# The first batch's mirror image added by the transfer that brings it, and transfers moved between engines, in a fused FFT and two-layer-pair kernel

## Chip, cores and metric

The kernel runs on one core of a Trainium2 chip. The metric is device microseconds of that core for one execution. Five engines take part: PE (TensorE, matrix products; PEld in the profile is its loading of weights), DVE (VectorE), ACT (ScalarE), POOL (GpSimd) and SP (SyncE, which only issues transfers here). Each engine works through its own list of instructions in order; a transfer (DMA) is issued by one engine's list and carried by 16 shared DMA engines. SP and ACT issue through one kind of queue, POOL through another.

## What is computed

The input x is 4 batches of 3008 rows by 256 columns, all float32. The parts of the reference that matter:

```
X = np.fft.fft(x, axis=1);  X = np.fft.fft(X, axis=2);  x = X.real      # (4, 3008, 256)
h = x @ w_in;   r = np.maximum(h, 0.0);  x = (r * r) @ w_out            # 256 -> 2048 -> 256
h = x @ w_in2;  x = (h * np.cos(h)) @ w_out2                            # 256 -> 2048 -> 256
```

The weights of both layer pairs arrive as float64 and are turned into pairs of float32r numbers (a high and a low part) on the chip. A product is then three matmuls: high by high, high by low, low by high.

## The kernel before

The transform along the rows uses its symmetries. For each batch and each of three row tiles t (128 partitions) two arrays of 128x1024 float32 (512 KB each) are loaded: one of row pairs a, and one of their mirror images b. `fold_steps` (line 230) then works in place on DVE: `mirrored` adds b to a (one 128x1024 instruction); two `eo` steps write sums and differences of even and odd parts (128x512 each); two `half` steps (128x512 each) write the next level; `hi` copies one half of the result into a float32r tile dh on ACT, `lo` writes the remainder dl on DVE; two `quarter` steps (128x256 each) and a second `hi` and `lo` do the other half. PE multiplies dh and dl by cosine and sine tables (`transform`, line 305; tables `tabs`, six tiles of 752 or 756 KB, loaded by POOL at line 206 with a conversion to float32r). A middle column of 128 rows goes the same way in small (`load_128`, `fold_128`, `job_128`). `finish` and `finish_first` turn the products into the rows z of the first layer's input (ACT, DVE, POOL) and store them to DRAM; the first two blocks of batch 0 stay on the chip as xh and xl.

The columns' transform is folded into the first layer's weights: `conv_w1` converts a chunk of w_in in eight steps (ACT and DVE), `dft_w1` multiplies it by the table cs on PE (line 416), `split_w1` splits the product into wah and wal.

Layer pair 1 runs in blocks of up to 512 pairs of tokens (12 blocks) by 16 slices of the hidden dimension: `l1_mm1` (line 527, six matmuls), `l1_add` (DVE: one multiply-add and two sums), `l1_act` (ACT: three passes), `l1_lo` (POOL, four instructions, line 557), `l1_mm2` (line 569, twelve matmuls, three steps later). Batches 1 to 3 are loaded, folded and transformed between those steps. The tables' tiles serve as landing place of the next batch's x in between, so the tables are loaded again for each batch (`reload_tab`, by POOL). Layer pair 2 works on 24 halves of blocks with eight steps each: `l2_mm1` (line 621), range reduction and cosine on ACT and DVE, `l2_lo` on POOL (line 660), `l2_mm2` (line 672); `l2_out` copies the sums out of PSUM, one half by ACT and one by DVE into one tile o, and stores both by SP.

The order of all this is written out by hand: every step is an entry `at(time, step, name)`; the dictionary `TIMES` (line 71) overrides the times of named entries, and the entries are issued in order of time. The time is only a sort key; what counts is the order that results on each engine. Before the first entry that runs on PE, for instance, SP issues the two halves of the first chunk of w_in, the middle column and the six arrays of batch 0 in one go, and POOL issues cs and all six tables. In the steady part POOL issues the loads of z (`load_z`), of the second layer's input (`load_o`), of the converted second weights (`load_w2`) and of the tables between its `l1_lo` and `l2_lo` instructions; SP issues everything else.

Of the kernel before, what the change touches and what calls it, by code (L numbers as in the profile page):

```python
# [10 lines left out]
F32 = mybir.dt.float32  # L11
# [5 lines left out]
AF = mybir.ActivationFunctionType  # L17
ALU = mybir.AluOpType
# [3 lines left out]
P = 128  # L22
# [8 lines left out]
NT = 3  # L31
# [5 lines left out]
BLK = 512  # L37
# [7 lines left out]
HALVES = [(2 * c + n * w, w) for c, w in BLOCKS for n in range(2)]  # L45
# [12 lines left out]
TW = (2 * J_A, EES + J_EE + 1)  # L58
# [15 lines left out]
class Order:  # L74
# [5 lines left out]
    def at(self, t, fn, name=None):  # L80
        self.ops.append((TIMES.get(name, t), len(self.ops), fn))

# [6 lines left out]
def f32(ap):  # L89
    return ap.bitcast(F32)  # L90
# [3 lines left out]
def kernel(ctx: ExitStack, tc: tile.TileContext, x, x128, cs, tab0, tab1, w_in1, w_out1, w_in2, w_out2, out):  # L94
    nc = tc.nc
# [10 lines left out]
    at = od.at  # L106
# [12 lines left out]
    def buf(tag, name, dt=F32, pool=work, bufs=1, shape=(P, 2, BLK)):  # L119
        return pool.tile(list(shape), dt, name=name, tag=tag, bufs=bufs)  # L120
# [35 lines left out]
    def from_f64(st, hi, lo, sh=None):  # L156
# [36 lines left out]
        def lower():  # L193
            r, unit = (w1.bitcast(F32), 2.0 ** -20) if middle is None else (middle, 2.0 ** -36)
            v.scalar_tensor_tensor(out=lo, in0=r, scalar=unit, in1=got["a"].bitcast(F32), op0=ALU.mult, op1=ALU.mult)

        return [size, guard, mask, merge, rest, power] + [join] * (middle is None) + [lower]


    raws, dat, jobs = {}, {}, {}  # L200
    tabs = [[buf(f"t{i}{t}", f"t{i}{t}", F32R, fft, 1, (P, 2, TW[i])) for t in range(NT)] for i in range(2)]
    cs_sb = []
    u128 = [buf(f"u128{p}", f"u128{p}", F32R, fft, 1, (P, 4, NT, B)) for p in "hl"]

    def load_tab(i, t):
        nc.gpsimd.dma_start(out=tabs[i][t], in_=(tab0, tab1)[i][t])

    def reload_tab(i, t):
        tabs[i][t] = buf(f"t{i}{t}", f"t{i}{t}", F32R, fft, 1, (P, 2, TW[i]))
        load_tab(i, t)  # L210

    def load_cs():
        cs_sb.extend(buf(f"cs{p}", f"cs{p}", F32R, fft, 1, (P, 2, D)) for p in "hl")
        for p, src in zip(cs_sb, cs):
            nc.gpsimd.dma_start(out=p, in_=src.rearrange("(k p) d -> p k d", p=P))

    def load_x(b, t, bufs):
        raws[b, t] = bufs
        for i, r in enumerate(bufs):
            nc.sync.dma_start(out=r, in_=x[b, t, i].rearrange("p a e d -> p (a e d)").rearrange("p (h n) -> p h n", h=2))  # L220

    def tt(out, in0, in1, op):
        nc.vector.tensor_tensor(out=out, in0=in0, in1=in1, op=op)  # L223

    PM = (ALU.add, ALU.subtract)
# [4 lines left out]
    def fold_steps(b, t):  # L230

        x = {}

        def views():
            ra, rb = raws.pop((b, t))
            x["a"], x["b"] = ra, rb
            x["eo"] = units(rb, "p (e a d) -> p e a d", e=2, a=4)

            x["f"] = units(ra, "p (i a b d) -> p i a b d", i=2, a=2, b=2)
            x["fv"] = units(ra, "p (a b d) -> p a b d", a=4, b=2)  # L240

            x["g"] = units(rb, "p (i a d) -> p i a d", i=4, a=2)

            x["src"] = (units(ra, "p (a n) -> p a n", a=4)[:, 1:3], units(rb, "p (a n) -> p a n", a=4)[:, 0:2])

        def mirrored():
            views()
            tt(x["a"], x["a"], x["b"], ALU.add)

        def eo(i):  # L250
            ab = units(x["a"], "p (a e d) -> p a e d", a=4, e=2)
            tt(x["eo"][:, i], ab[:, :, 0], ab[:, :, 1], PM[i])

        def half(i):
            tt(x["f"][:, i], x["eo"][:, :, 0::2], x["eo"][:, :, 1::2], PM[i])

        def quarter(i):
            tt(x["g"][:, i], x["fv"][:, 0:4:3, 0], x["fv"][:, 0:4:3, 1], PM[i])

        def hi(i):  # L260
            if i == 0:
                x["p"] = [buf(f"d{p}", f"d{p}", F32R, fft, NT, (P, 2, 2, 2 * P)) for p in "hl"]
                dat[b, t] = [p.rearrange("p a b (u d) -> p (a b u) d", d=P) for p in x["p"]]
            nc.scalar.activation(x["p"][0][:, i], x["src"][i], AF.Copy)  # L264

        def lo(i):
            tt(x["p"][1][:, i], x["src"][i], f32(x["p"][0])[:, i], ALU.subtract)

        return [mirrored] + [lambda i=i, fn=fn: fn(i) for fn, i in (
            (eo, 0), (eo, 1), (half, 0), (half, 1), (hi, 0), (lo, 0), (quarter, 0), (quarter, 1), (hi, 1), (lo, 1))]  # L270
# [11 lines left out]
    def load_128():  # L282
        raws["mid"] = scratch(2, NT, 4, B)
        nc.sync.dma_start(out=raws["mid"], in_=x128)
# [114 lines left out]
    def load_w1(c, bufs):  # L399
        for k, st in enumerate(bufs):  # L400
            nc.sync.dma_start(out=st.rearrange("p h n -> p (h n)").rearrange("p (n t) -> p n t", t=2),
                              in_=src_in(w_in1, k, c * FCH * P, FCH * P))
            wi[c, k] = st.rearrange("p h n -> p (h n)").rearrange("p (n t) -> p n t", t=2)
# [89 lines left out]
    def load_w2(name, c):  # L493
        parts = w_chunk("a" if name == "in" else "b")
        for p, src in zip(parts, w2_dram[name, c]):
            nc.gpsimd.dma_start(out=p, in_=src)
        (wi2 if name == "in" else wo2).append(parts)
# [16 lines left out]
    def load_z(k, i):  # L514
        c, w = BLOCKS[k]
        if i == 0:
            load_zb(k, x_buf())
        nc.gpsimd.dma_start(out=xt[1, k][i][:, :, :w], in_=z_dram[i][:, :, c:c + w].rearrange("i p w -> p i w"))
# [86 lines left out]
    def load_o(k):  # L605
        c, w = HALVES[k]
        parts = x_buf()
        for p, o in zip(parts, o_dram):
            nc.gpsimd.dma_start(out=p[:, :, :w], in_=o[:, :, c:c + w].rearrange("m p w -> p m w"))
        xt[2, k] = parts  # L610
# [64 lines left out]
    def l2_out(k):  # L675
        c, w = HALVES[k]
        o = buf("AB"[k % 2] + "0", "o")
        a = accs.pop((2, k))
        nc.scalar.activation(o[:, 0, :w], a[:, 0, :w], AF.Copy)
        nc.vector.tensor_copy(o[:, 1, :w], a[:, 1, :w])  # L680
        for m in range(2):
            nc.sync.dma_start(out=out[m][:, c:c + w], in_=o[:, m, :w])
# [42 lines left out]
    def fold(times, b, t):  # L725
        got = []

        def step(j):
            if j == 0:
                got.extend(fold_steps(b, t))  # L730
            got[j]()

        for j, when in enumerate(times):
            at(when, lambda j=j: step(j), ("fold", b, t, j))
# [15 lines left out]
    for t in range(NT):  # L750
        fold([-80 + t + 0.05 * j for j in range(7)] + [0.02 + 0.1 * t + 0.01 * j for j in range(4)], 0, t)
        for i, job in enumerate(JOBS[::2]):
            at(-79.5 + t + 0.01 * i, lambda t=t, i=i, job=job: start_first(job, ps_a, f"acc{i}", (t,)), ("T", 0, i, t))
        at(-79.45 + t, lambda t=t: job_128(0, (t,)), ("job_128", 0, t))
        at(-78.7 + 0.01 * t, lambda t=t: load_tab(1, t), ("tab", 1, t))
# [17 lines left out]
    t = 0.4  # L773
# [3 lines left out]
    for key in KEYS:  # L777
        span = 1.5
        if isinstance(key, tuple):
            c, k = key  # L780
            convert(t, span, key, lambda c=c, k=k: conv_w1(c, k))
            if k:
                end = t + span
                at(end, lambda c=c: dft_w1(c), ("dft", c))
                at(end + 0.1, lambda c=c: split_w1(c), ("split", c))
                at(end + 0.8, lambda c=c: load_wc(c), ("load_wc", c))
                if c < NCH - 1:
                    at(end + 0.01, lambda c=c: load_w1(c + 1, pair("B", I32)), ("load_w1", c + 1))
        else:
            convert(t, span, key, lambda f=key: conv_wo1(f))  # L790
            if key < NF - 4:
                at(t + span, lambda f=key + 4: load_wo1(f, buf(f"A{f // 2 % 2}", "wo", I32)), ("load_wo1", key + 4))
        t += span


    for b, (load, start, gap, t1, gap1) in {1: ((14, 21, 21.6), 26, 4, 38.4, 1.5), 2: ((53, 53.5, 54), 54, 4.6, 68, 2), 3: ((76, 76.5, 77), 78, 4.6, 92, 2)}.items():
        for t in range(NT):
            at(load[t], lambda b=b, t=t: load_x(b, t, staged(t)), ("load_x", b, t))
            fold([start + gap * t + gap / 11 * j for j in range(11)], b, t)
        for i in range(2):  # L800
            for t in range(NT):

                at(start + gap * ((i * NT + t) // 2 + 1) + 0.1, lambda i=i, t=t: reload_tab(i, t), ("tab", b, i, t))
        for i, job in enumerate(JOBS):
            def begin(b=b, job=job):
                jobs[b, job] = ps_h.tile([P, 2, BLK], F32, name="h")
                transform(job, jobs[b, job], lhs_of(b), P)

            at(t1 + gap1 * i + 0.2, begin, ("T", b, *job))
            finish(t1 + gap1 * i + 0.9, b, job, lambda b=b, job=job: jobs[b, job], lambda: pair("B", F32R), 0.3)  # L810
# [175 lines left out]
```

## Time and profile before

| | us |
|---|---|
| median of three runs | 1945.47 |
| lowest and highest run | 1945.16, 1946.25 |
| the profiled execution's own time | 1946.22 |
| its span, first to last instruction | 1944.4 |
| PE busy in the span | 1893.9 |
| DVE, ACT, POOL busy | 1361.7, 1482.8, 1139.8 |

The span is 1.8 us shorter than the time of the same execution; the rest lies around it. A busy time is the sum of an engine's instructions. The granted clock of a stretch is the share of full speed at which the throttle let TensorE run: 1.00 is 2.4 GHz, 0.50 is 1.2 GHz. Its mean over the span is 0.993.

### The profile page before, as it was taken

To read this page: it belongs to the slowest core of one execution; us is meant where nothing else is said; L and a number is where in the kernel's file an instruction comes from. 1 tells how busy PE (TensorE), PEld (TensorE's weight loads), DVE (VectorE), ACT (ScalarE), POOL (GpSimd) and SP (SyncE) were. 2 spreads that over 40 slices of the span, in tenths; PEclk is the share of its full clock that TensorE was granted. 3 is DMA by queue.
4 is the path that set the end of the run, shared out by engine and by line. 5 is a ranking of instruction groups with operands and counts; after the bars stand their busy time and mean duration, and the time that the engine had idled before them with its cause. 6 is when DMAs were issued, how large, how long until landed. Compare 5 with 4: busy or idle time off the path is not lost.

```text
span 1944.4 us, 23842 instructions
## 1 busy us (share of the span) xinstructions
PE 1893.9 (97%) x8544; PEld 1572.1 (81%) x8544; DVE 1361.7 (70%) x1563; ACT 1482.8 (76%) x1537; POOL 1139.8 (59%) x1105
## 2 busy tenths in 40 slices
PE   6799999999999999999999999999999999999999
PEld 4577787777888888888888888888888888888887
DVE  7789858769576776765766666666666666666666
ACT  3788777768788888887877777777777777777776
POOL 1567887768787778786544444444444444444442
PEclk8899999999999999999999999999999999999999
DMA  7544443443443343436111111121111111111110
GB/s 274 171 150 136 145 128 140 151 139 113 150 143 132 123 140 117 141 123 192 55 33 32 32 32 33 33 59 37 33 32 33 33 32 44 51 33 33 32 32 21
DMA packets 76153, 173.22 MB, mean 89 GB/s; under 512 B 9072, under 2 KB 32640, under 8 KB 76036
## 3 DMA queue, kind: packets, MB, share of 16 engines
q1 hardware_dynamic: 50692, 108.32, 16.4%
q0 software_dynamic: 25344, 63.39, 11.2%
q8 instruction: 67, 1.10, 0.2%
q14 instruction: 50, 0.41, 0.1%
HBM read 112.90 MB, written 58.79 MB: 88 GB/s over the span
## 4 chain that ended last, share of the span: by engine, by line
PE 77%; DVE 3%; issue 1%; ACT 1%; DVEq 0%; ACTq 0%
PE acc L672 26%; PE h L621 18%; PE acc L569 16%; PE acc L621 9%; PE h L527 8%; PE h L310 1%; DVE s L223 1%; DVE inT L223 1%; DVE u L534 0%; DVE r L635 0%; ACT s L545 0%; ACT s L544 0%; ACT gh L547 0%; ACT dh L264 0%; DVE ol L223 0%
## 5 line engine op out<-in xcount | busy, mean ns | idle before, releaser
L660 POOL TENSOR_TENSOR gl<-r,gh 128x1024 fp32r<-128x1024 f32 (+2 forms) x189 | 445.0, 2355 | 541.5 <-ACT gh L653 471.7
L557 POOL TENSOR_TENSOR gl<-s,gh 128x256 fp32r<-128x256 f32 (+2 forms) x768 | 593.7, 804 | 206.2 <-ACT gh L547 168.7
L635 DVE SCALAR_TENSOR_TENSOR r<-n,h 128x1024 f32<-128x1024 int32 (+2 forms) x129 | 154.7, 1199 | 219.2 <-ACT n L627 199.7
L544 ACT ACTIVATE s<-s 128x1024 f32<-128x1024 f32 (+2 forms) x192 | 199.6, 1040 | 106.6 <-DVE s L223 103.0
L223 DVE TENSOR_TENSOR s<-u,h 128x512 f32<-128x512 f32 (+2 forms) x384 | 242.7, 673 | 23.3 <-POOL gl L557 1.3
L627 ACT ACTIVATE n<-h 128x1024 int32<-128x1024 f32 (+2 forms) x129 | 130.3, 1010 | 160.9 <-PE h L621 160.8
L569 PE MATMUL acc<-gl,wbh 128*128 128x512 f32 (+2 forms) x768 | 237.4, 389 | 4.5 <-POOL gl L557 4.4
L569 PE MATMUL acc<-gh,wbh 128*128 128x512 f32 (+2 forms) x768 | 238.2, 392 | 2.1 <-DVE ol L223 2.1
L635 DVE SCALAR_TENSOR_TENSOR r<-n,r 128x1024 f32<-128x1024 int32 (+2 forms) x192 | 233.4, 1216 | 6.6
L569 PE MATMUL acc<-gh,wbl 128*128 128x512 f32 (+2 forms) x768 | 235.3, 388 | 0.0
L534 DVE SCALAR_TENSOR_TENSOR u<-zb,wc,h 128x512 f32<-128x512 f32 (+2 forms) x192 | 140.6, 732 | 132.5 <-PE h L527 131.5
L643 ACT ACTIVATE r<-r,halfpi 128x1024 f32<-128x1024 f32 (+2 forms) x192 | 218.4, 1137 | 6.2
L545 ACT ACTIVATE s<-s 128x1024 f32<-128x1024 f32 (+2 forms) x192 | 200.5, 1044 | 6.1
L547 ACT ACTIVATE gh<-s 128x1024 fp32r<-128x1024 f32 (+2 forms) x192 | 200.5, 1044 | 6.1
L672 PE MATMUL acc<-gh,wbh 128*128 128x512 f32 (+2 forms) x768 | 202.8, 386 | 0.0
L672 PE MATMUL acc<-gh,wbl 128*128 128x512 f32 (+2 forms) x768 | 202.8, 386 | 0.0
L672 PE MATMUL acc<-gl,wbh 128*128 128x512 f32 (+2 forms) x768 | 202.8, 386 | 0.0
L621 PE MATMUL h<-xh,wah 128*128 128x512 f32 (+2 forms) x516 | 199.0, 386 | 1.1 <-DVE r L223 1.1
L642 ACT ACTIVATE r<-r 128x1024 f32<-128x1024 f32 (+2 forms) x192 | 198.2, 1032 | 1.9 <-DVE r L635 1.8
L621 PE MATMUL h<-xl,wah 128*128 128x512 f32 (+2 forms) x516 | 198.9, 386 | 0.0
L621 PE MATMUL h<-xh,wal 128*128 128x512 f32 (+2 forms) x516 | 198.9, 386 | 0.0
L653 ACT ACTIVATE gh<-r 128x1024 fp32r<-128x1024 f32 (+2 forms) x192 | 197.1, 1027 | 0.4 <-DVE r L223 0.4
(144 smaller groups left out, 3344.1 us busy)
## 6 DMA issues: line engine op xcount, KB each, us to landing
inT<-x_in SPq DMA_DIRECT2D x18, 512.0 KB, 6.6
t<-tab_in POOLq DMA_DIRECT2D x12, 756.0 KB, 5.9
t<-tab_in POOLq DMA_DIRECT2D x12, 752.0 KB, 5.9
oh<-oh SPq DMA_DIRECT2D x16, 512.0 KB, 2.9
ol<-ol SPq DMA_DIRECT2D x16, 512.0 KB, 4.6
xh<-oh POOLq DMA_DIRECT2D x16, 512.0 KB, 4.2
xl<-ol POOLq DMA_DIRECT2D x16, 512.0 KB, 5.1
y_out<-o SPq DMA_DIRECT2D x32, 256.0 KB, 3.7
```

Of the source, the lines that this page charges most:

```text
L223: nc.vector.tensor_tensor(out=out, in0=in0, in1=in1, op=op)
L544: nc.scalar.activation(s[:, :, :w], s[:, :, :w], AF.Relu)
L545: nc.scalar.activation(s[:, :, :w], s[:, :, :w], AF.Square)
L547: nc.scalar.activation(hi[:, :, :w], s[:, :, :w], AF.Copy)
L557: nc.gpsimd.tensor_tensor(out=lo[:, n, cols], in0=s[:, n, cols], in1=f32(hi)[:, n, cols], op=ALU.subtract)
L569: nc.tensor.matmul(accs[1, k][m][:, n, :w], wt, g[:, n, :w], start=begin and i == 0, stop=end and i == 2)
L621: nc.tensor.matmul(a[:, j, :w], st, mv[:, m, :w], start=m == 0 and q == 0, stop=m == 1 and q == 2)
L635: nc.vector.scalar_tensor_tensor(out=r[:, :, :w], in0=n[:, :, :w], scalar=-c, in1=src[:, :, :w], op0=ALU.mult, op1=ALU.add)
L642: nc.scalar.activation(r[:, :, :w], r[:, :, :w], AF.Abs)
L643: nc.scalar.activation(r[:, :, :w], r[:, :, :w], AF.Sin, bias=halfpi, scale=-1.0)
L660: e.tensor_tensor(out=lo[:, :, :w], in0=r[:, :, :w], in1=f32(hi)[:, :, :w], op=ALU.subtract)
L672: nc.tensor.matmul(accs[2, k][:, m, :w], w_out_t([c[part] for c in wo2], f, m), g[:, j, :w], start=f == 0 and q == 0, stop=f == NF - 1 and ...
```

## The change

Seven edits, in the order of the diff:

1. `TIMES` is replaced. The names are nearly the same; the order changes most among the first 150 or so entries, and later by a few places here and there.
2. The tables are copied once from their input arrays to tensors in DRAM (`copy_tab`, six transfers by SP, spread over steps 9 to 17 of the first layer pair); `reload_tab` loads them from there by SP and not by POOL.
3. For batch 0, `load_x` loads only the first array of each tile; tile 1's by ACT, the others by SP. Step 0 of the fold becomes a transfer by POOL that adds the mirror image from DRAM to what is in SBUF (`accum_op`). Other batches add on DVE as before.
4. For batch 0 the two `half` steps become four `some` steps of 128x256, of which two come ahead of the first `hi` and two after the first `lo`.
5. The middle column is loaded by ACT; of the first chunk of w_in the second half is loaded by ACT.
6. `load_w2`, `load_z` and `load_o` are issued by SP and not by POOL.
7. `l2_out` copies into two tiles, one for ACT and one for DVE; the last half's second store is issued by ACT.

```diff
-TIMES = {'load_cs': -91.459, ('load_w1', 0): -91.03, ('tab', 0, 0): -90.601, 'load_128': -90.171,
...
+TIMES = {'load_128': -97.418, ('tab', 0, 0): -96.836, 'load_cs': -96.254, ('load_x', 0, 1): -95.673, 'fold_128': -95.091, ('load_w1', 0): -94.509,
...
+    tab_dram = {(i, t): dram.tile([P, 2, TW[i]], F32, name=f"tab{i}{t}") for i in range(2) for t in range(NT)}
+
+    def copy_tab(i, t):
+        nc.sync.dma_start(out=tab_dram[i, t], in_=(tab0, tab1)[i][t])
+
     def reload_tab(i, t):
         tabs[i][t] = buf(f"t{i}{t}", f"t{i}{t}", F32R, fft, 1, (P, 2, TW[i]))
-        load_tab(i, t)
+        nc.sync.dma_start(out=f32(tabs[i][t]), in_=tab_dram[i, t])
...
+    def queues(n):
+        return (nc.sync, nc.sync if n else nc.scalar)
...
     def load_x(b, t, bufs):
         raws[b, t] = bufs
-        for i, r in enumerate(bufs):
-            nc.sync.dma_start(out=r, in_=x[b, t, i].rearrange("p a e d -> p (a e d)").rearrange("p (h n) -> p h n", h=2))
+        for i, r in enumerate(bufs if b else bufs[:1]):
+            (nc.sync if b or t != 1 else nc.scalar).dma_start(out=r, in_=x_half(b, t, i))
...
         def mirrored():
             views()
-            tt(x["a"], x["a"], x["b"], ALU.add)
+            if b:
+                tt(x["a"], x["a"], x["b"], ALU.add)
+            else:
+                nc.gpsimd.dma_start(out=x["a"], in_=x_half(b, t, 1), accum_op=ALU.add)
...
+        def some(ia):
+            i, a = ia
+            tt(x["f"][:, i, a], x["eo"][:, a, 0::2], x["eo"][:, a, 1::2], PM[i])
+
+        halves = [(some, (0, 1)), (some, (1, 0))] if b == 0 else [(half, 0), (half, 1)]
+        others = [(some, (0, 0)), (some, (1, 1))] if b == 0 else []
         return [mirrored] + [lambda i=i, fn=fn: fn(i) for fn, i in (
-            (eo, 0), (eo, 1), (half, 0), (half, 1), (hi, 0), (lo, 0), (quarter, 0), (quarter, 1), (hi, 1), (lo, 1))]
+            (eo, 0), (eo, 1), *halves, (hi, 0), (lo, 0), *others, (quarter, 0), (quarter, 1), (hi, 1), (lo, 1))]
...
-        nc.sync.dma_start(out=raws["mid"], in_=x128)
+        nc.scalar.dma_start(out=raws["mid"], in_=x128)
...
     def load_w1(c, bufs):
-        for k, st in enumerate(bufs):
-            nc.sync.dma_start(out=st.rearrange("p h n -> p (h n)").rearrange("p (n t) -> p n t", t=2),
+        for e, k, st in zip(queues(c), range(2), bufs):
+            e.dma_start(out=st.rearrange("p h n -> p (h n)").rearrange("p (n t) -> p n t", t=2),
...
-            nc.gpsimd.dma_start(out=p, in_=src)
+            nc.sync.dma_start(out=f32(p), in_=src)
...
-        nc.gpsimd.dma_start(out=xt[1, k][i][:, :, :w], in_=z_dram[i][:, :, c:c + w].rearrange("i p w -> p i w"))
+        nc.sync.dma_start(out=f32(xt[1, k][i])[:, :, :w], in_=z_dram[i][:, :, c:c + w].rearrange("i p w -> p i w"))
...
-            nc.gpsimd.dma_start(out=p[:, :, :w], in_=o[:, :, c:c + w].rearrange("m p w -> p m w"))
+            nc.sync.dma_start(out=f32(p)[:, :, :w], in_=o[:, :, c:c + w].rearrange("m p w -> p m w"))
...
-        o = buf("AB"[k % 2] + "0", "o")
+        os = [buf("AB"[k % 2] + str(m), "o", shape=(P, 2, BLK))[:, 0, :w] for m in range(2)]
         a = accs.pop((2, k))
-        nc.scalar.activation(o[:, 0, :w], a[:, 0, :w], AF.Copy)
-        nc.vector.tensor_copy(o[:, 1, :w], a[:, 1, :w])
-        for m in range(2):
-            nc.sync.dma_start(out=out[m][:, c:c + w], in_=o[:, m, :w])
+        nc.scalar.activation(os[0], a[:, 0, :w], AF.Copy)
+        nc.vector.tensor_copy(os[1], a[:, 1, :w])
+        for m, e in enumerate((nc.sync, nc.scalar if k == len(HALVES) - 1 else nc.sync)):
+            e.dma_start(out=out[m][:, c:c + w], in_=os[m])
```

In the new order the first entries on each engine are these. SP issues the first half of w_in, then the first arrays of tiles 0 and 2. ACT issues the middle column and the first array of tile 1, does the copy of `fold_128` that waits for the middle column, and then issues the second half of w_in. POOL issues table (0, 0) and the two parts of cs, then the adding transfer of tile 1, that of tile 0, the tables (0, 2) and (0, 1), the adding transfer of tile 2, and the three tables of the other kind. On DVE `fold_128` comes before the conversion of w_in, the conversion runs without a fold step in it, and the folds of tiles 0, 1 and 2 follow, each up to its first `lo`, with the split of the first weights in the fold of tile 1. The rest of the folds (the other `some` steps, `quarter`, second `hi` and `lo`) comes between the steps of `finish_first`.

## Rows read from the trace of the kernel before

**Rows 1.** Windows: stretch, length, engines' busy us (instructions), PEclk, DMA share, GB/s.

```profile
0.00:9.20 9.20, 0.00 (x0) 0.00 (x0) 3.49 (x8) 2.57 (x3) 5.00 (x12) 1.00 0.87 278
9.20:28.50 19.30, 14.71 (x60) 9.35 (x60) 16.87 (x31) 4.30 (x7) 0.00 (x0) 1.00 1.01 384
28.50:38.00 9.50, 4.75 (x29) 3.54 (x28) 6.66 (x15) 4.06 (x10) 0.69 (x1) 0.68 0.18 54
38.00:60.00 22.00, 16.37 (x101) 12.08 (x99) 17.76 (x31) 13.18 (x21) 9.74 (x13) 0.81 0.55 178
60.00:110.00 50.00, 43.96 (x169) 33.72 (x168) 41.36 (x67) 38.86 (x45) 29.45 (x36) 0.91 0.55 173
110.00:500.00 390.00, 375.19 (x1731) 306.91 (x1730) 308.27 (x405) 298.20 (x314) 296.04 (x377) 1.00 0.43 140
500.00:1939.00 1439.00, 1437.90 (x6461) 1206.00 (x6460) 966.63 (x1009) 1121.02 (x1138) 798.89 (x667) 1.00 0.21 66
1939.00:1944.40 5.40, 0.98 (x5) 0.51 (x3) 0.66 (x1) 0.57 (x1) 0.00 (x0) 0.90 0.26 92
```

**Rows 2.** Timeline of PE up to 60 us: start, busy, line, [idle before, releaser].

```profile
9.24 0.76 PE L416 MATMUL h<-wih,csh 128*128 128x512 f32 x1 [9.24 <-DMA csh<-cs_in]
...
30.66 0.96 PE L310 MATMUL acc<-t,dh 64*128 64x376 f32 x8 [2.12 <-ACT dh L264]
...
55.34 0.47 PE L527 MATMUL h<-xh,wah 128*128 128x512 f32 x1 [3.72 <-DVE s L223]
```

**Rows 3.** Timeline of DVE, 10 to 40 us.

```profile
10.22 0.43 DVE L170 TENSOR_SCALAR f64t<-f64t 128x512 f32<-128x512 f32 x1 [0.73 <-ACT f64t L166]
...
11.02 0.79 DVE L223 TENSOR_TENSOR zb<-zb 128x48 f32<-128x48 f32 x6
12.11 0.21 DVE L223 TENSOR_TENSOR u128l<-zb,u128h 128x48 fp32r<-128x48 f32 x1 [0.31 <-ACT u128h L296]
12.24 1.22 DVE L223 TENSOR_TENSOR inB<-inB,inB 128x1024 f32<-128x1024 f32 x1
...
18.96 1.22 DVE L223 TENSOR_TENSOR in<-in 128x1024 f32<-128x1024 f32 x1
...
26.07 3.87 DVE L223 TENSOR_TENSOR in<-in 128x1024 f32<-128x1024 f32 x5
30.63 0.69 DVE L223 TENSOR_TENSOR dl<-in,dh 128x512 fp32r<-128x512 f32 x1 [0.69 <-ACT dh L264]
```

**Rows 4.** Groups of DVE instructions up to 60 us: count, busy, mean ns, idle before.

```profile
L223 DVE TENSOR_TENSOR inB<-inB 128x512 f32<-128x512 f32 x4 | 2.6, 686 | 0.0
L191 DVE SCALAR_TENSOR_TENSOR inA<-inA 128x512 f32<-128x512 uint32 x2 | 1.4, 685 | 0.0
L191 DVE SCALAR_TENSOR_TENSOR wo<-wo 128x512 f32<-128x512 uint32 x1 | 1.2, 1225 | 0.0
L223 DVE TENSOR_TENSOR inB<-inB 128x256 f32<-128x256 f32 x2 | 0.8, 406 | 0.0
```

**Rows 5.** DMA issues of the whole span: queue, count, KB each, median us to landing.

```profile
t<-tab_in POOLq DMA_DIRECT2D x12, 756.0 KB, 5.9
...
xh<-oh POOLq DMA_DIRECT2D x16, 512.0 KB, 4.2
...
in<-x_in SPq DMA_DIRECT2D x4, 512.0 KB, 12.6
...
inA<-w_in SPq DMA_DIRECT2D x2, 512.0 KB, 4.9
...
y_out<-o SPq DMA_DIRECT2D x4, 242.0 KB, 2.1
```

**Rows 6.** Waits, whole span: who waited for whom, us in total, times, longest.

```profile
PE acc L569 <- POOL gl L557: 4.4, 7, 1.4
PE h L310 <- DMA t<-tab_in: 1.1, 1, 1.1
ACT mid L166 <- DMA mid<-w_in: 7.1, 3, 4.6
```

**Rows 7.** Groups of POOL instructions, whole span: count, busy, mean ns, idle before.

```profile
L609 POOL DMA_DIRECT2D xh<-oh x24 | 17.7, 737 | 0.0
L206 POOL DMA_DIRECT2D t<-tab_in x24 | 13.4, 566 | 0.0
L518 POOL DMA_DIRECT2D xh<-zh x11 | 8.1, 739 | 0.0
```

**Rows 8.** Timeline, the last 5 us.

```profile
1940.02 0.57 ACT L679 ACTIVATE o<-acc 128x484 f32<-128x484 f32 x1 [4.86 <-PE acc L672]
1940.62 1.03 SPq L682 DMA_DIRECT2D y_out<-o  x2
1940.62 0.66 DVE L680 COPY o<-acc 128x484 f32<-128x484 f32 x1 [4.26 <-ACT o L679]
```

More of the change, by code (lines that the diff above doesn't have):

```diff
@@ L215, in load_cs, with x_half @@
             nc.gpsimd.dma_start(out=p, in_=src.rearrange("(k p) d -> p k d", p=P))
+    def queues(n):
+        return (nc.sync, nc.sync if n else nc.scalar)
+    def x_half(b, t, i):
+        return x[b, t, i].rearrange("p a e d -> p (a e d)").rearrange("p (h n) -> p h n", h=2)
     def load_x(b, t, bufs):
         raws[b, t] = bufs
-        for i, r in enumerate(bufs):
-            nc.sync.dma_start(out=r, in_=x[b, t, i].rearrange("p a e d -> p (a e d)").rearrange("p (h n) -> p h n", h=2))
+        for i, r in enumerate(bufs if b else bufs[:1]):
+            (nc.sync if b or t != 1 else nc.scalar).dma_start(out=r, in_=x_half(b, t, i))
     def tt(out, in0, in1, op):
@@ L750 @@
     for t in range(NT):
-        fold([-80 + t + 0.05 * j for j in range(7)] + [0.02 + 0.1 * t + 0.01 * j for j in range(4)], 0, t)
+        fold([-80 + t + 0.05 * j for j in range(7)] + [0.02 + 0.1 * t + 0.01 * j for j in range(6)], 0, t)
         for i, job in enumerate(JOBS[::2]):
@@ L793 @@
         t += span
+    for n, (i, t) in enumerate((i, t) for i in range(2) for t in range(NT)):
+        at(9.37 + n, lambda i=i, t=t: copy_tab(i, t), ("copy_tab", i, t))
     for b, (load, start, gap, t1, gap1) in {1: ((14, 21, 21.6), 26, 4, 38.4, 1.5), 2: ((53, 53.5, 54), 54, 4.6, 68, 2), 3: ((76, 76.5, 77), 78, 4.6, 92, 2)}.items():
```

2 lines of the change are left out of this document (1 added, 1 removed).

## Prediction, before the run

> **What bounds the kernel now.** I read the stretches first [rows 1]. The reader is to see that PE is all but full from 500 us on: of 1439 us it rests 1.1. So nothing that the change does to layer pair 2 (loads of its input and weights by SP, two tiles o) can win more than that there. What is left to win lies in four places: the first 9.2 us, in which PE waits for its first operands [rows 2]; 9.2 to 60 us, where PE rests 4.6, 4.7 and 5.6 us; 60 to 110 us with 6.0 us; 110 to 500 us with 14.8 us. To these comes the clock: at 0.68, 0.81 and 0.91 of full speed in three stretches up to 110 us, which is 9.5 x 0.32 + 22 x 0.19 + 50 x 0.09 = 11.7 us of lost full-speed time, some of it while PE had nothing to do.
>
> Then the waits of PE up to 60 us [rows 2]: the fold of the third tile (dh, 2.12 us), and at 55 us a sum on DVE (3.72 us). Both end in DVE work, and the timeline of DVE shows why [rows 3]: from 10 to 31 us it goes from one instruction to the next, and its gaps (0.73, 0.31, 0.69 us) are waits for ACT, not for a transfer. The two mirror sums at 18.96 and 26.07 us have no idle time before them at all, so their data had landed. The transfer engines are full as well in this stretch (share 1.01, 384 GB/s [rows 1]), but the one landing that the view of DMA issues shows for x, 12.6 us after an issue at 3.4 to 5.4 us [rows 5], is at 16 to 18 us, ahead of both sums. So DVE bounds the start, the transfers being the next thing behind it.
>
> **The change part by part, up to 60 us.** The sum is made for the moment at which DVE gets to the work that ends PE's wait at 55 us.
>
> The three mirror sums leave DVE: 3 x 1.22 = 3.66 us less [rows 3]; the one at 12.24 us counts too, for it stood inside the conversion of w_in that PE waits for.
>
> Two half steps of 0.69 us become four of 0.41 us [rows 4]: 1.64 against 1.37, so 3 x 0.27 = 0.8 us more in all by 55 us, although 0.55 us less per tile stands ahead of the first high part.
>
> The middle column's fold (0.79 + 0.21 us and a wait of 0.31 us [rows 3]) goes to before the conversion, where DVE has nothing else to do until w_in has landed 4.9 us after its issue [rows 5]: 1.3 us less. ACT issues the second half of w_in behind its share of that fold; that half is wanted only some 5 us later, when the first is converted, so I count nothing; if the middle column came late, both would wait.
>
> In the old order the mirror sum of tile 1 filled DVE's time between the first high and low part of tile 0. Now the low part follows at once and DVE waits for ACT as it does at 30.63 us [rows 3]: 0.7 us more.
>
> The first half of w_in now shares the transfer engines with two other queues rather than one. At a half of 384 GB/s its 524 kB take 2.7 us, at a third 4.1 us, so it is late by 0 to 1.4 us; I take the middle, 0.7 us.
>
> The adding transfers are not in the trace. Each can be issued only after its first array has landed, and POOL's list stands still meanwhile; behind it stand the tables (0, 2) and (0, 1) and the next adding transfer, for which PE and DVE wait in turn. Nearest rows: 512 KB on POOL's queue in a quiet stretch take 4.2 us, 512 KB in the crowded start 12.6 us [rows 5]. Below 4.2 us I see no reason to go, as the same bytes are read from DRAM. Tile 0 is wanted at about 16 us (16.4 us less 1.3 us, plus 0.7 us). Its first array is second in SP's list and may be there at about 7 us, so the image lands between 12 and 20 us: late by 0 to 4 us. The queue is emptier than before, since the tables are held back behind it; I take 0.5 us. Tile 2 is wanted at about 24 us and should be there.
>
> Sum: -3.66 + 0.8 - 1.3 + 0.7 + 0.7 + 0.5 = -2.3 us, between -3.5 and about +3 us.
>
> The Trainium skill, page "DMA: Bandwidth & Descriptors", section "Rules for kernel authors", says that an accumulating DMA reads its destination and writes it later. By that each adding transfer moves its 524 kB once more; at 384 GB/s that is an estimate of 1.4 us each, 4.1 us for the three, and the forecast would be nearer to 1942 us. No row of before shows such a transfer, so the trace neither bears this out nor speaks against it.
>
> The clock: an earlier third tile shortens the pauses around 28 to 37 us, after which the clock stood at 0.68 and 0.81 [rows 1]. That can give back up to 3 us, or take 1 us if a new pause opens; I take -0.5 us.
>
> **From 60 us to the end.** 60 to 110 us: 6.0 us of rest and 4.5 us of clock [rows 1], in a new order of conversions, sums and stores. I can't work that out instruction by instruction; it may win or lose 4 us, and I take -0.7 us because the DVE work of the start arrives earlier.
>
> 110 to 500 us: the wait for a table, 1.1 us [rows 6], should go, because SP issues the table without standing behind POOL's subtractions. POOL no longer spends 0.57 us on each of 18 reloaded tables and 0.74 us on each part of z [rows 7]; but PE waits for POOL only 4.4 us in all, part of it before 110 us [rows 6], so I take -0.4 us. Against this, six copies of the tables (DRAM to DRAM, about 750 KB each; nearest row 5.9 us each for a load [rows 5]) run in a stretch with a DMA share of 0.43 [rows 1], so there is room; where one lies ahead of a staged load of w_in, ACT waits longer than the 7.1 us that it waits already in three places [rows 6]: 0 to 5.9 us each, I take 0.3 us in all. SP's loads stand behind its stores now, which wait for ACT and POOL: 0 to 3 us, I take 0.3 us, as z is asked for some four steps ahead. Together -0.9 us, between -4 and +4 us.
>
> 500 to 1939 us: 24 loads of the second layer's input leave POOL (0.74 us for each part [rows 7]); PE does not wait there, so nothing.
>
> The end: ACT's copy ends at 1940.6 us and only then DVE's begins, for the two share a tile [rows 8]. With two tiles DVE starts beside ACT and the second store leaves 0.6 us earlier; its 2.1 us to landing [rows 5] stay. -0.6 us.
>
> Total: -2.3 - 0.5 - 0.7 - 0.9 - 0.6 = -5.0 us. The profiled execution's own time is 1946.2 us (span 1944.4 and 1.8 around it), which gives 1941.2 us; it stands 0.7 us above the median of the runs, so I forecast 1940.5 us. What a measurement of this kernel can tell from no change is about 0.2%, 3.9 us.
>
> **Rivals.**
>
> The start is set by bytes. For it: the transfer engines' share of 1.01 up to 28.5 us [rows 1]; the same bytes must come, and w_in, x and three tables are needed whatever the order. Against it: the two sums without idle time before them [rows 3]. Then DVE waits for the images for as long as it saves, the start gives 0, and the end and the middle about -1.5 us: 1944 us.
>
> A larger gain. PE's pauses become so short that the clock stays at 1.00 and the DVE lead carries through the conversions: half of the 11.7 us of clock, half of the 6.0 us of rest between 60 and 110 us, -2.3, -0.9 and -0.6 us: about -12.6 us, 1933 us. For it: the clock is below 1.00 only in the stretches where PE rests [rows 1]. Against it: the waits at 55 us and later come from the whole chain of ACT, DVE and POOL, and the change takes only 2 to 3 us out of it.
>
> Slower: the adding transfers come late. Place: POOL's list between 7 and 25 us. If tile 0's first array takes the 12.6 us of [rows 5] and the adding transfer as long again, tile 0 is there at about 27 us and not at 16; the folds behind it and the tables held back on POOL shift with it: -5.0 + 11 = +6 us, 1951.5 us. It decides against the change once that image lands later than 21 us, for a delay of 5 us eats the whole gain. For it: POOL issues while DVE converts, and the two hinder each other, as the same instruction takes 0.69 us alone and 1.23 us beside POOL's work [rows 4]. The Trainium skill's page "DMA: Bandwidth & Descriptors", section "SWDGE vs HWDGE vs iDMA", gives a reason for such a delay: GpSimd writes the descriptors of its transfers into SBUF, and DVE can lock it out there while it runs in a two-port mode. The trace of before has POOL's issues over by 6 us, beside at most two DVE instructions, and so does not test that. Against: POOL needs 0.6 to 0.7 us for an issue [rows 7], and DVE's instructions here are shorter than that or alike.
>
> **How the numbers follow.** Forecast 0.50, its own range 1936 to 1943.5 us; start set by bytes 0.22; larger gain 0.13; slower 0.15. Of the forecast's 0.50 some 0.05 lies within 0.2%. Faster by over 0.2%: 0.45 + 0.13 = 0.58; within: 0.05 + 0.22 = 0.27; slower: 0.15. The range from 1932 to 1948.5 us leaves out the lower half of the larger gain (0.06) and the larger part of the slower case (0.1).
>
> **What would show it.** DVE's first `eo` step on tile 0 right behind the conversion, near 16 us, without a wait for a transfer, shows the images in time; a wait there for x or a POOL release shows the rival. The last low part of the three first tiles should end near 29 us and not 31.3 us. The granted clock from 28 to 60 us should be no lower than before. PE's wait for a table should be gone. DVE's last copy should start beside ACT's. The prediction is wrong if the start gains but 60 to 110 us gives it back, or if loads of z or of tables, now on SP, appear among PE's waits.

## The result and the profile after

The changed kernel takes 1927.71 us (median of four runs, 1927.07 to 1927.88), beside it the kernel before 1945.86 us (four runs). The ratio is 0.9905, between 0.9888 and 0.9922: 18 us faster, where 5 were forecast and 1932 us was the lower end of the range. The span fell by 19.1 us, from 1944.4 to 1925.3.

The windows of the kernel after, with the stretches and columns of [rows 1] (the last boundary follows the earlier end):

```profile
0.00:9.20 9.20, 0.00 (x0) 0.00 (x0) 2.71 (x12) 2.32 (x4) 2.33 (x7) 1.00 0.81 284
9.20:28.50 19.30, 13.21 (x54) 7.96 (x54) 14.07 (x26) 4.67 (x7) 5.43 (x8) 0.91 1.10 331
28.50:38.00 9.50, 5.59 (x36) 3.59 (x34) 6.86 (x17) 3.85 (x9) 0.00 (x0) 1.00 0.59 219
38.00:60.00 22.00, 16.13 (x96) 11.33 (x96) 16.39 (x33) 12.71 (x22) 10.66 (x14) 0.82 0.49 150
60.00:110.00 50.00, 45.83 (x182) 35.61 (x183) 44.71 (x71) 42.41 (x49) 29.42 (x37) 0.94 0.65 208
110.00:500.00 390.00, 384.90 (x1820) 320.11 (x1819) 300.37 (x415) 306.46 (x324) 291.66 (x368) 1.00 0.44 152
500.00:1920.00 1420.00, 1420.00 (x6358) 1191.99 (x6357) 956.17 (x996) 1108.33 (x1125) 735.14 (x572) 1.00 0.20 66
1920.00:1925.30 5.30, 0.99 (x5) 0.52 (x3) 0.66 (x1) 0.57 (x1) 0.00 (x0) 1.00 0.27 94
```

PE's rest (length less PE's busy time) against [rows 1] is to be read stretch by stretch: up to 60 us 24.2 before and 25.1 now; 60 to 110 us 6.0 and 4.2; **110 to 500 us 14.8 and 5.1**; after that 1.1 and 0; at the end 4.4 and 4.3. That is 11.9 us. The other 7.2 us are PE's own busy time, 1893.9 and 1886.7. The mean clock rose from 0.993 to 0.996, which is 0.007 x 1944 = 13.6 us of lost full-speed time before and 0.0044 x 1925 = 8.5 now, 5 us less. Part of that fell into PE's rests; counted only while PE was busy, it is 11.0 and 7.3 us. So 3.7 of the 7.2 us are clock, and the other 3.5 I can't assign. About half of the gain lies between 110 and 500 us, where batches 1 to 3 are folded beside layer pair 1, not in the start.

PE's waits from 110 to 500 us (us in total, times, longest), first the kernel before:

```profile
PE h L527 <- DVE s L223: 5.9, 5, 1.9
PE acc L569 <- POOL gl L557: 2.6, 5, 1.0
PE acc L569 <- DVE ol L223: 2.1, 2, 1.6
PE h L310 <- DVE s L223: 1.6, 1, 1.6
PE h L310 <- DMA t<-tab_in: 1.1, 1, 1.1
```

and the kernel after:

```profile
PE h L550 <- DVE s L235: 2.4, 3, 1.1
PE acc L592 <- POOL gl L580: 1.3, 2, 1.0
PE acc L592 <- DVE ol L235: 0.7, 1, 0.7
```

The wait for a table went, as forecast. But the largest change is in waits for DVE (9.6 to 3.1 us), though the change leaves DVE's work in this stretch alone but for small shifts of order. Why DVE was late shows in the timeline of the kernel before, around 355 and 422 us (PE, DVE and POOL; start, busy):

```profile
361.70 0.50 PE L527 MATMUL h<-xh,wah 128*128 128x512 f32 x1 [0.63 <-DVE s L223]
365.25 0.50 PE L527 MATMUL h<-xh,wah 128*128 128x512 f32 x1 [1.88 <-DVE s L223]
...
432.93 0.49 PE L527 MATMUL h<-xh,wah 128*128 128x480 f32 x1 [1.86 <-DVE s L223]
...
355.70 3.87 DVE L223 TENSOR_TENSOR inT<-inT 128x512 f32<-128x512 f32 x2
...
422.79 7.41 DVE L223 TENSOR_TENSOR inT<-inT 128x512 f32<-128x512 f32 x1
430.73 0.73 DVE L534 SCALAR_TENSOR_TENSOR u<-zb,wc,h 128x512 f32<-128x512 f32 x1
...
354.98 0.58 POOL L206 DMA_DIRECT2D t<-tab_in  x1
355.58 2.83 POOL L557 TENSOR_TENSOR gl<-s,gh 128x256 fp32r<-128x256 f32 x4
...
421.35 0.74 POOL L518 DMA_DIRECT2D xl<-zl  x1
422.11 2.83 POOL L557 TENSOR_TENSOR gl<-s,gh 128x256 fp32r<-128x256 f32 x4
424.91 1.95 POOL L346 TENSOR_TENSOR inB<-z,inB 128x378 fp32r<-128x378 f32 x2
426.83 2.81 POOL L557 TENSOR_TENSOR gl<-s,gh 128x256 fp32r<-128x256 f32 x4
```

A fold sum of 128x512, 0.69 us in quiet [rows 4], takes 7.41 us. It starts while POOL runs subtractions right behind the issue of a load of z, and ends only 0.6 us after the last of POOL's ten (429.6 us). POOL's own run is undisturbed, 0.71 us for each subtraction that writes gl. `l1_add` stands behind that sum on DVE, and PE waits for it. The event at 355 us has a price in clock too, for PE rests 2.5 us between 360 and 366 us and the granted clock is 0.57 in the next 4 us (1.00 before):

```profile
360.00:366.00 6.00, 3.49 (x14) 2.28 (x13) 5.41 (x8) 4.43 (x6) 3.70 (x7) 1.00 0.40 124
366.00:370.00 4.00, 4.00 (x11) 2.69 (x11) 3.90 (x6) 3.94 (x5) 2.07 (x3) 0.57 0.86 338
```

The same sum (the 44th of its kind) and the one behind it in the kernel after, where no issue stands on POOL:

```profile
412.11 2.01 DVE L235 TENSOR_TENSOR inT<-inT 128x512 f32<-128x512 f32 x2
414.04 0.74 DVE L557 SCALAR_TENSOR_TENSOR u<-zb,wc,h 128x512 f32<-128x512 f32 x1
...
410.29 3.28 POOL L580 TENSOR_TENSOR gl<-s,gh 128x256 fp32r<-128x256 f32 x4 [1.26 <-ACT gh L570]
413.53 2.42 POOL L369 TENSOR_TENSOR inB<-z,inB 128x378 fp32r<-128x378 f32 x2
```

The two sums take 2.01 us, and POOL's subtractions give way, 0.82 us each and not 0.71. DVE and POOL take turns.

### The profile page after: what moved, and what is told of

Same layout as the page of the kernel before. It is cut to its first block, busy times and chain, and to the rows that moved or that the text cites. A ratio compares the mean times of both kernels' runs of the same rounds, so it can differ in the third digit from the quotient of the medians.

```text
span 1925.3 us, 23825 instructions
## 1 busy us (share of the span) xinstructions
PE 1886.7 (98%) x8544; PEld 1571.1 (82%) x8544; DVE 1341.9 (70%) x1566; ACT 1481.3 (77%) x1537; POOL 1074.6 (56%) x1004
## 4 chain that ended last, share of the span: by engine, by line
PE 81%; DVE 1%; issue 0%; ACT 0%; DVEq 0%; ACTq 0%
PE acc L695 27%; PE h L644 18%; PE acc L592 18%; PE acc L644 9%; PE h L550 9%; PE h L333 1%; DVE s L235 0%; DVE inT L235 0%; DVE u L557 0%; DVE ol L235 0%; ACT oh L618 0%; DVE o L703 0%; ACT o L702 0%; DVEq L235 0%; DVE dl L235 0%
```

## The experiments

**Theory M**: an issue on POOL next to its subtractions makes POOL keep DVE's sums of two SBUF arrays out for several instructions; that is the stretch from 110 to 500 us. Rivals: **N**, the new order does it; **S**, the shorter start does it; **L**, what stood behind POOL's subtractions simply came late. Times of the kernel before beside these runs (medians): 1945.3 to 1946.8 us.

**Which part of the change pays.** The changed kernel with its loads of tables, z, o and w2 on POOL again, without the copies:

```diff
-        nc.sync.dma_start(out=f32(tabs[i][t]), in_=tab_dram[i, t])
+        load_tab(i, t)
...
-        nc.sync.dma_start(out=f32(xt[1, k][i])[:, :, :w], in_=z_dram[i][:, :, c:c + w].rearrange("i p w -> p i w"))
+        nc.gpsimd.dma_start(out=xt[1, k][i][:, :, :w], in_=z_dram[i][:, :, c:c + w].rearrange("i p w -> p i w"))
```

> The changed kernel with only the later loads (z, second layer's input, second weights, reloaded tables) issued by POOL again, no table copies; new order and new start kept. Theory M (a transfer issued by POOL holds up the two-input sums on DVE and POOL's own subtractions, and that is where the 13 us between 110 and 500 us came from): 1938 to 1942 us, single DVE sums of several us again. Rival N (the new order did it): below 1931 us.

1940.0 us, ratio 0.9969 (0.9956 to 0.9981): 12.3 us of the 18 are gone, and the 8 us pair of sums is back (417.79 us). The counterpart, the kernel before with only these loads on SP:

> The kernel before with only the later loads and the table copies by SP; old order, old start, old end. Theory M: 1931 to 1936 us, no DVE sum above 2 us between 110 and 500 us. Rival N: 1943 to 1948 us, as the old order stays. Rival S (the start did it, the middle only shows it later): within 3 us of before.

1936.8 us, 0.9955 (0.9940 to 0.9970): 8.5 us in the old order. Its PE rests 5.5 us from 110 to 500 us and no sum is long. A little less than M said, but N falls: the loads pay without the new order. The changed kernel with the mirror sums on DVE and all first arrays loaded plainly:

> The changed kernel with the three mirror sums of batch 0 on DVE again, each right before the tile's first even/odd step, and all six arrays loaded by SP and ACT. Theory M: within 3 us of the changed kernel (1925 to 1931 us), since the first 80 us of the two traces lie within 2 us of each other. Rival S: 1935 us or more.

1934.1 us, 0.9942 (0.9927 to 0.9957): the adding transfers are worth 6.4 us here, twice what M alone allowed. All of it comes in the start: PE runs the same matmuls in the same order as in the changed kernel, so each can be set beside its fellow; here it is 6.1 us behind at 40 us and 6.4 us at the end. One reason shows in the lines: without them ACT gets the second half of w_in at 15.9 us, not 13.2, and the last of the first three low parts is at 35.1 us, not 29.5.

```profile
15.92 0.66 ACT L166 ACTIVATE f64t<-inA 128x512 f32<-128x512 f32 x1 [6.36 <-DMA inA<-w_in]
...
35.06 0.69 DVE L235 TENSOR_TENSOR dl<-in,dh 128x512 fp32r<-128x512 f32 x1 [0.69 <-ACT dh L276]
```

The new order without either (the two edits above together):

> The changed kernel's order (with the four smaller fold steps, first transfers by two engines and the split o tile), but the mirror sums on DVE and all reloads on POOL without copies: only what edits 1, 4, 5 and 7 are worth. If the parts add up, 18.1 - 12.3 (reloads) - 6.4 (mirror) leaves -0.6 us: about 1946.5 us, between 1943 and 1950. Rival (the order itself pays and the other edits only let it): 1936 to 1942 us.

1945.5 us, 0.9994 (0.9985 to 1.0004): nothing as a whole. The parts add up: 12.3 for the reloads and 6.4 for the mirror are 18.7, against 18.1 for the whole.

**The adding transfer in the old order**, for batch 0, first where the old order puts it. On POOL's list the first one then stands behind three of the six tables, not behind all six as the expectation says:

```diff
-            tt(x["a"], x["a"], x["b"], ALU.add)
+            nc.gpsimd.dma_start(out=x["a"], in_=x_half(b, t, 1), accum_op=ALU.add)
```

> The kernel before, in its old order, with only the adding transfers: batch 0's mirror images added by POOL's transfer in place of DVE's three sums. All loads where they were. In the new order the adding transfers were worth 6.4 us. Theory S (it pays because DVE bounds the start): 3.7 us of sums leave DVE, and with 524 KB less in the queue ahead of each other transfer the start shortens by 3 to 6 us: 1940 to 1943 us. Rival O (it pays only in the new order, since in the old one the adding transfers stand behind six tables on POOL and come late): no faster, 1945 to 1952 us, with DVE waiting for the first tile's image after 16 us.

1948.2 us, 1.0009 (1.0000 to 1.0018): no faster, as rival O said. DVE waits 5 us for the first image:

```profile
20.39 2.62 DVE L226 TENSOR_TENSOR inB<-inB 128x512 f32<-128x512 f32 x4 [5.04 <-DMA inB<-x_in]
```

Then with one table ahead of it (three entries of `TIMES`):

> The kernel before in its old order with the adding transfers, which now stand on POOL ahead of the tables (0, 2) and (0, 1) and not behind all six. Theory: with the images not held up behind the tables the adding transfer pays in the old order too, 3 to 6 us: 1940 to 1943 us. Rival: it pays only where the conversion of the first weights comes ahead of the folds and the first arrays are asked for first, as in the new order: 1944 to 1950 us.

1943.7 us, 0.9987 (0.9977 to 0.9996), between the theory's range and the rival's: the first image is there at 16.5 us, and the edit pays 2.5 us (0.0013 of the time). It is not issued earlier (9.1 us, against 8.8 in the version above); with one table ahead of it and not three it lands 7.4 us after its issue and not 11.6. So it needs its place on POOL's list, and it pays most where the new order otherwise starts late (35.1 us above, against 30.6 before [rows 3]).

```profile
16.49 2.62 DVE L226 TENSOR_TENSOR inB<-inB 128x512 f32<-128x512 f32 x4 [0.87 <-DMA inB<-x_in]
```

**Which load does it.** The changed kernel with only the tables, only z, or only o and w2 on POOL:

> The changed kernel with only the reloaded tables (18 loads) issued by POOL again, from their input arrays, without the copies; z, o and w2 stay on SP. Theory M (a transfer issued by POOL next to its subtractions makes POOL run without a gap and hold back DVE's sums of two arrays, whose results PE waits for): one of the four long sums of the kernel before stood beside a table (355.7 us, 3.9 us), three beside z, so 2 to 5 us of the 12.3 us come back: 1930 to 1933 us, and a DVE sum of over 2 us next to a table's issue. Rival L (loads that stand behind POOL's subtractions simply come late): only the wait for a table comes back, 1.1 us: about 1929 us, with PE waiting for a table and no long DVE sum. Rival N (the order does it): 1927.7 us.

1938.9 us, 0.9958 (0.9943 to 0.9973). Four sums take 2.7 to 3.3 us, each beside a table's issue.

> The changed kernel with only the loads of z (layer pair 1's input) issued by POOL again. Theory M: 6 to 11 us come back, 1934 to 1939 us, with DVE sums of 2.5 to 8 us right after an issue of z on POOL, in the stretches where batches 1 and 2 are folded. Rival L: PE never waited for z in the kernel before, so nothing: 1927.7 us within 1 us. Rival N: 1927.7 us too.

1935.0 us, 0.9941 (0.9926 to 0.9955). One sum is long, 7.39 us, behind an issue of z at 410 us.

> The changed kernel with only the loads of the second layer pair's input and weights on POOL again. Both theories: PE has no idle time after 500 us and DVE's sums there take h from PSUM, so nothing: 1927.7 us within 2 us. Rival (the issues on POOL cost wherever they stand): 1931 to 1937 us.

1928.3 us, 0.9907 (0.9892 to 0.9921). Tables cost 11.2 us alone, more than forecast, z 7.3, all together 12.3: not a sum; a paragraph below shows that part of the first and last figure lies elsewhere. L falls with z, for which PE never waited; o and w2 cost nothing, where DVE has no fold sums and PE no rest.

**What about an issue does it.** 40 needless issues (4 KB, DRAM to DRAM) in the changed kernel, one at each load of a table or of z:

```diff
+    def idle_load():
+        spent.append(dram.tile([P, 8], F32, name=f"spent{len(spent)}"))
+        nc.gpsimd.dma_start(out=spent[-1], in_=tab0[0][:, 0, :8])
```

> The changed kernel with all its loads on SP, plus at each of the 40 places of a load of a table or of z one needless transfer of 4 KB from DRAM to DRAM, issued by POOL, that nobody waits for. Theory M: the issue alone does it, whatever it carries: 1934 to 1941 us, with DVE sums of over 2 us beside these issues. Rival L: the loads themselves are as early as in the changed kernel, so nothing beyond 1 us: 1927 to 1929 us, although POOL spends 20 to 30 us more on issuing. Rival B (the bytes on POOL's queue, or the conversion of type on the way, do it): 1927 to 1929 us too.

1933.3 us, but wide, 1928.0 to 1936.4; ratio 0.9926 (0.9903 to 0.9949), which overlaps the changed kernel's own interval (0.9888 to 0.9922). The trace is plain: the sum at 412.61 us takes 7.17 us of the 7.77, behind an issue that brings nothing anyone needs. L and B don't give such a sum.

```profile
412.61 7.77 DVE L242 TENSOR_TENSOR inT<-inT 128x512 f32<-128x512 f32 x2
...
411.17 0.52 POOL L217 DMA_DIRECT2D spent<-tab_in  x1
411.70 2.83 POOL L588 TENSOR_TENSOR gl<-s,gh 128x256 fp32r<-128x256 f32 x4
```

The same places with memsets on POOL in place of the issue, 20 of them and then 5:

> The changed kernel plus, at the same 40 places, 20 small memsets of 128x4 on POOL in place of the needless transfer: POOL's time without an issue. Theory M in its wide form (any time taken from POOL there lets its subtractions pile up and run without a gap): as much as with the empty issues in proportion to the time they take, some 4 to 12 us: 1932 to 1940 us. Theory M in its narrow form (it is the writing of the transfer's descriptors, beside DVE): within 2 us of 1927.7 us, and no DVE sum of over 2 us beside the memsets. Rival L: 1927.7 us.

1975.1 us, 1.0148 (1.0133 to 1.0163). The dose was four issues' time, and neither form of M had the size: PE waits for POOL's `gl` itself, 19.3 us in this stretch alone, and no sum is long (largest 1.76 us). At one issue's dose:

> As the kernel with 20 memsets at each of 40 places, but with 5 of them: 5 x 0.105 = 0.53 us of POOL, which is what one needless issue took (0.527 us in the kernel with empty issues). Theory M in its narrow form (POOL's subtractions keep DVE's two-input sums out for their whole run only when they start right behind an issue): no sum longer than its normal time by more than 1.1 us, and at most the cost of POOL's time itself, 0 to 3 us: 1927 to 1931 us. In its wide form (POOL's time decides): as with the empty issues, 1932 to 1935 us.

1930.1 us, 0.9912 (0.9897 to 0.9927). In time this can't be told from the empty issues, for the intervals overlap; in the trace it can, for DVE and POOL take turns behind the memsets:

```profile
413.19 1.83 DVE L242 TENSOR_TENSOR inT<-inT 128x512 f32<-128x512 f32 x2
...
411.74 0.73 POOL L217 MEMSET spent<- 128x4 f32 x5
412.49 3.83 POOL L588 TENSOR_TENSOR gl<-s,gh 128x256 fp32r<-128x256 f32 x4
```

All loads on POOL and a memset behind each issue:

> The changed kernel with all loads of tables, z, o and w2 on POOL again (the kernel that measured 1940.0 us), plus one memset of 128x4 on POOL behind each of these issues, so that no subtraction starts right behind an issue. More work on POOL. Theory M, narrow: the long DVE sums go, and with them most of the 12 us: 1928 to 1933 us. Theory M, wide, and rival L (late loads): no faster than without the memsets: 1939 to 1943 us, with DVE sums of 3 to 8 us as before.

1940.3 us, 0.9967 (0.9954 to 0.9980): no help, so it isn't that a subtraction follows directly. The narrow form as I had put it falls:

```profile
415.65 8.01 DVE L238 TENSOR_TENSOR inT<-inT 128x512 f32<-128x512 f32 x2
...
414.20 0.74 POOL L545 DMA_DIRECT2D xl<-zl  x1
414.94 0.12 POOL L546 MEMSET spent<- 128x4 f32 x1
415.00 2.83 POOL L585 TENSOR_TENSOR gl<-s,gh 128x256 fp32r<-128x256 f32 x4
```

An issue with idle time behind it (a memset that waits until the transfer out of its tile has landed):

> The changed kernel plus, at the 40 places, one needless 4 KB transfer out of SBUF issued by POOL, with a memset behind it that has to wait until it has landed: an issue with idle time behind it. If POOL keeps DVE out only when it goes from an issue into its subtractions without any idle time, no sum takes over 1.1 us more than normal, though there are 40 issues; the time is set by POOL's lost 2 to 3 us at each place instead, 1940 to 1980 us with PE waiting for gl. If an issue alone is enough, idle time or not, sums of 3 to 8 us appear as with the empty issues.

1982.4 us, 1.0175 (1.0154 to 1.0196), from POOL's lost time; but with 40 issues no sum is long:

```profile
L245 DVE TENSOR_TENSOR inT<-inT x63: 412/1016/1765, 175.1 to 513.3; 128x512 f32<-128x512 f32 x36, 128x256 f32<-128x256 f32 x18, 128x1024 f32<-128x1024 f32 x9
```

All 17 traces say the same. I took the 81 fold sums of batches 1 to 3 in each (`inT`, `dl`), and for each that starts within one of POOL's subtractions, what stood ahead of it in that run of POOL (a run ends at a pause of 0.1 us) and by how much the sum exceeds its shortest like in the same trace:

| POOL's run, up to the sum | sums | over by more than 1.1 us | largest excess, us |
|---|---|---|---|
| no issue in it | 853 | 0 | 0.82 |
| memsets in it, no issue | 48 | 0 | 0.60 |
| begins 0.1 us or more behind an issue | 107 | 0 | 0.60 |
| goes on from an issue without a pause | 80 | 31 | 6.74 |

It is not the length of POOL's run: 811 of the 1008 sums in the first three rows had over 2 us of it still ahead of them, and none was late. In the last row the shares are 5 of 12 in the kernel before and 3 of 10 with the memsets between. The place counts: of the 35 sums that start in the first subtraction behind the issue (or behind its memset) 26 are late, of the 45 that start further on 5. Why not all 35, the traces don't tell.

**How much of the time that is.** All these kernels run the same matmuls in the same order, so PE's lag in the profiled executions, matmul by matmul, shows where the time goes. Behind the changed kernel (us; a column names the time at which the matmul starts there):

| on POOL in addition | 120 us | 300 us | 500 us | last |
|---|---|---|---|---|
| tables, z, o and w2 | 4.7 | 5.2 | 13.3 | 13.6 |
| tables | 4.9 | 5.4 | 12.4 | 12.7 |
| z | 0.0 | 0.0 | 4.4 | 4.4 |
| 40 needless issues | 1.0 | 1.3 | 7.4 | 7.3 |
| 5 memsets in place of each | 0.7 | 0.6 | 1.6 | 1.6 |

Between 300 and 500 us the issues cost 4.4 to 8.1 us and the same time in memsets 1.0 us, and the large steps come right behind the long sums. In the old order the kernel before is 2.2 us ahead of the one with its loads on SP at 300 us and 9.6 us behind at 500. But the first two rows are 4.7 and 4.9 us late by 120 us, although with the tables alone POOL's list is the same as in the changed kernel up to 200 us; 2.3 of those 4.9 us are there by 60 us, where every engine's list is the same. So up to 5 of the 12.3 us are not the effect of issues beside fold sums, and the runs don't show what they are.

**A version beyond the changed one.** ACT issues the second half of w_in before the middle column's copy:

> The changed kernel, with ACT issuing the second half of the first weights ahead of its copy of the middle column and not behind it. In the changed kernel ACT waited 3.5 us for that half. If that wait is on the path that sets the end of the start, 1 to 3 us: 1924.5 to 1927 us. Rival: the transfers of the start bound it, the half takes its bytes from the middle column and from x, and nothing is won: 1927.7 us within 1 us.

1928.6 us, 0.9903 (0.9886 to 0.9919): nothing. The half comes 0.4 us earlier (12.83 us), the first image 0.5 us later, which fits the rival: what one transfer gains another loses.

```profile
12.83 0.67 ACT L166 ACTIVATE f64t<-inA 128x512 f32<-128x512 f32 x1 [3.25 <-DMA inA<-w_in]
```

No version beat the changed kernel.

## Why the prediction was wrong

**The step that failed** is the 110 to 500 us term, in the words "PE waits for POOL only 4.4 us in all ... so I take -0.4 us". It sized POOL's issues by PE's waits for POOL. Their price was in the waits for DVE shown above, one engine further on, and the timeline of DVE there, with its 7.41 us sum, was never read; I looked at DVE only up to 40 us [rows 3]. The term was -0.9 us; PE's rest there fell by 9.7 us. The six copies and SP's queueing, +0.3 us each, show nowhere among PE's waits.

**Clock**, -0.5 us up to 60 us: by the prediction's own sum 7.2 us were lost there before and 5.7 are now, -1.5 us; over the whole span the loss fell by about 5 us. Beyond 66 us the clock now no longer falls: 86 to 93 and 366 to 370 us stood at half speed before, the first after rests of PE for `l1_add` (0.7 us) and for ACT's `wcrow` (1.7 us), the second after the rests for `l1_add` shown above. So most of the clock's gain lay behind pauses that I had not looked at.

**Start**, -2.3 us for the matmul at 55.34 us [rows 2]: it starts at 56.14 us now, 0.8 us later. The parts:

```profile
56.14 0.76 PE L550 MATMUL h<-xh,wah 128*128 128x512 f32 x1 [1.75 <-DVE s L235]
...
13.21 0.67 ACT L166 ACTIVATE f64t<-inA 128x512 f32<-128x512 f32 x1 [3.51 <-DMA inA<-w_in]
...
9.68 0.91 POOL L264 DMA_DIRECT2D in<-x_in  x1 [6.30 <-DMA in<-x_in]
10.26 1.21 POOL L264 DMA_DIRECT2D inB<-x_in  x1
...
18.63 2.09 DVE L235 TENSOR_TENSOR inB<-inB 128x512 f32<-128x512 f32 x4 [0.62 <-DMA inB<-x_in]
...
29.46 0.69 DVE L235 TENSOR_TENSOR dl<-in,dh 128x512 fp32r<-128x512 f32 x1 [0.70 <-ACT dh L280]
```

The second half of w_in, counted at nothing, cost ACT 3.5 us, and DVE's conversion ended 1.5 us later than before (18.0 against 16.5 us). The image of tile 0 landed at 18.6 us and not near 16.5: POOL stood still for 6.3 us until tile 1's first array had landed, so that tile 0's adding transfer left at 10.3 us. That DVE waited only 0.6 us for it (forecast 0.5) is luck, as the late conversion hid the rest. The last low part ended at 30.15 us (forecast near 29). So the fold gained 1.2 us and not 2.3, and the matmul at 55 us hung on other work: DVE had waited 2.25 us for POOL's gl before 51.4 us. The gain shows later: the 100th matmul of `l1_mm2` starts at 106.7 us, 2.9 us earlier than before. The adding transfers were worth 6.4 us within the new order, and in the old one lost 1.5 or won 2.5 us; my sum did not see that they hang so on their place and on the bytes ahead of them.

**60 to 110 us**, -0.7 us: 1.9 us less rest. **Tail**, -0.6 us: 0.1 us. With two tiles DVE's copy still waits for ACT's; why, I did not test:

```profile
1921.03 0.57 ACT L702 ACTIVATE o<-acc 128x484 f32<-128x484 f32 x1 [4.85 <-PE acc L695]
1921.63 0.66 DVE L703 COPY o<-acc 128x484 f32<-128x484 f32 x1 [4.26 <-ACT o L702]
```

The rivals: "start set by bytes" was half right (the start gave nothing by 60 us, and the half of w_in shows the bytes), "slower" did not occur (image at 18.6 us, before the 21 us at which it would decide), and "a larger gain" came nearest in time (1933 us), but by luck: of its 5.9 us of clock and 3.0 us of rest up to 110 us, 3.0 and 1.9 came, and the 9.7 us between 110 and 500 us it did not have.

Open: the 4.7 us by which the kernel with its loads on POOL is late at 120 us, and what makes an issue followed at once by subtractions different from a memset in the same place. Whether POOL's time by itself costs anything at one issue's dose isn't shown: with the five memsets the ratio is 0.9912 against 0.9905, within the noise.

## What to carry to other kernels

An engine's relief is not sized by who waits for that engine: list the stretched instructions of its neighbour too (longest against shortest of one form; here 7.41 against 0.69 us), then who waits for those. In this kernel loads issued by POOL in the middle of POOL arithmetic belonged on SP where DVE adds SBUF arrays at that time; elsewhere (o and w2, 1928.3 us) they cost nothing. An adding transfer needs its place ahead of what is not urgent, since the loads asked for before it delay its landing (7.4 or 11.6 us after the issue): the same edit moved the time by +1.5, -2.5 and -6.4 us in three places.

## What the hardware showed that was not expected

DVE and POOL take turns, as a rule: a DVE sum of two SBUF arrays was late by at most 0.82 us, about one subtraction. The Trainium skill, page "SBUF — State Buffer", section "SBUF: two separate sides", says that a DVE instruction with two SBUF inputs and a GpSimd instruction that reads SBUF compete for one port pair, that the first to start has it for its whole instruction and that the other blocks; the 1008 sums of the first three rows of the table agree. Behind an issue without a pause the sum waited for up to ten of POOL's instructions (7.41 us), which the rule, taken instruction by instruction, does not give. A memset between did not change it (3 of 10 late); idle time did (0 of 107).

The adding transfers moved their bytes at half rate at full engine share, first the kernel before, then after:

```profile
13.00:17.50 4.50, 1.85 (x4) 1.12 (x4) 4.20 (x8) 0.63 (x1) 0.00 (x0) 1.00 1.07 412
```

```profile
13.00:17.50 4.50, 2.02 (x4) 1.00 (x4) 3.22 (x7) 1.30 (x2) 2.11 (x4) 1.00 1.07 214
```

The packets say whose rate that is: those of the adding transfers (4096 bytes, on POOL's queue) took 0.33 us each, those of the same size on SP's and ACT's queues 0.16 and 0.17 us (medians, up to 28.5 us). The rule of the Trainium skill's page "DMA: Bandwidth & Descriptors", section "Rules for kernel authors", which the prediction cites, agrees with that: the same share, 214 and not 412 GB/s. They still paid in the new order, where they stand behind the first arrays and the second half of w_in comes 2.7 us earlier than without them. Their issue had no price of its own: it took POOL 0.9 to 1.6 us there, and the plain tables between them took 1.1 to 1.6.
